# Two transformer layers on one core: pace of the row maxima, order of some loads, last block's rows kept on chip, banks of the first scores

## Chip, cores and metric

The kernel runs on one core of a Trainium2 chip. The metric is the device time of one execution in microseconds. Times are medians of several runs; one further execution is profiled, and all traces below are of such executions.

## What is computed

Two pairs of layers on an input of 2048 rows and 640 columns, in float32. Each pair is an attention layer and an MLP, both added to their input, with the same weights in both pairs:

```python
x = x + A(layernorm(x))     # D = 640, 32 heads of 20, softmax over 2048 keys
x = x + B(layernorm(x))     # F = 1536, squared relu, two biases
...                         # once more

def A(x):
    qkv = (x @ wqkv).reshape(1, 2048, 3, 32, 20)
    p = softmax(einsum("bhqd,bhkd->bhqk", q, k) * 20 ** -0.5)
    return einsum("bhqk,bhkd->bhqd", p, v) @ wo

def B(x):
    h = x @ w1 + b1
    return where(h > 0, h, 0) ** 2 @ w2 + b2
```

## The kernel before

**Stages.** `layer` is called twice. Each call runs three stages one behind the other: `qkv` (the projections, by blocks of 512 rows), `attention`, and the output projection with the MLP (`add_heads` for four row blocks, then `mlp` for four). Most products are made of three products of float32r pieces ("high" and "low"). Between stages the pieces of q, k, v and of the weights lie in DRAM and come by DMAs issued on the SP queue, in the order of the program.

**Order.** All instructions are issued by a schedule written out in Python. Each engine works through its own instructions in that order, and waits where another engine or a DMA isn't done. PSUM has eight banks. Rings hand them out in turn: `ps_st` (banks 0 to 3) for scores, `ps_q` (0 to 3) for maxima and transposes in `qkv`, `ps_pj` (4 to 7) for projections, `sm_ring` (4, 5, 6) for maxima in the attention, `ps_all` (all eight) in the rest.

**Projections.** `qkv` goes through 72 chains, 40 for queries and keys (`UNITS`, by row block `tb` and position) and 32 for values, each of 15 products on both halves of the rows of the array. Between their matmuls it inserts other work, chosen by a model of the engines' time (`now`, with `READY` and 0.235 us for a step): transposes of the next row block (`turns`), and maxima of the first attention blocks. `step_rest` advances a generator that loads and normalises the next rows; when it hands over a `turns` generator, that is queued with the model time from which it may run. In layer two the rows of blocks 0 to 2 come turned through DRAM already; block 3 is loaded again (`second`, with `rows_of_block` and `prepare`: statistics of four rows, then normalising of four) and turned by TensorE. At the end of a value chain `end_v` copies the bank to `v` (line 377). When the last chain is two thirds through, the first four scores are issued (`for o in "abab"`).

**Attention.** 32 blocks `t` of four heads by 512 queries, each with 16 key tiles. The scores are made a second time by queries, ahead of use, to find each row's maximum: a matmul in `smax` (line 481) and a reduction on VectorE (line 493); the negated maxima go through DRAM into two rows of `q` (`mrows`, `mrows_load`; names `nm`, `mr`, `d_m`), where line 563 adds them into the score. Some maxima are taken in pairs during `qkv` ("double", line 510). The others are spread over the attention. It works in groups of eight key tiles; a group's order is a string of `ORDERS`, chosen by how many pairs of maxima it has to hold (12 to 16):

```python
12: "naambbmVanmbambVbmannabVnabnmabVabnmbanVbbmnanaVbmmbaanVbmbmnaaV",
```

`a` and `b` are scores of the two heads in the two halves of the array, with the exponential on ScalarE behind each (line 570); `m` and `n` are maxima in the two halves; `V` is the product with the values for one key tile (line 575). `pairs` chooses the number: it takes the pace at which the maxima of each block would be done in time, adds it to a debt, and takes whole pairs from the debt. The last block is done with scores two banks wide (`both_heads`, lines 1089 and 1096).

**Behind the attention.** `add_heads` has four row blocks of eight chains (line 293, 15 matmuls each); VectorE adds each to a row tile `x` (line 1164), which was loaded one block ahead. After each chain `side` runs one of the queued `steps`; they normalise and turn block 0 for the MLP: `turn_out` writes turned rows to `d_t`, `turn_in` loads them (`xnT<-d_t`) and splits them on ScalarE (line 1212) and VectorE or Pool (line 1213). The weights of the MLP are loaded there too: `loads` gives each block its own (w_1 has 15 slots of 512 KB at most, w_2 16). `mlp` adds the second product to its rows on VectorE (line 1260) and stores them; the last tile in two halves.

Of the kernel before, what the change touches and what calls it, by code (L numbers as in the profile page):

```python
# [11 lines left out]
ALU = mybir.AluOpType  # L12
# [13 lines left out]
NQB = S // QB  # L26
NG = H // 4
NKT = S // P
# [11 lines left out]
def tile_layers(  # L40
# [11 lines left out]
    nc = tc.nc  # L52
# [17 lines left out]
    def dma(eng, dst, src):  # L70

        if dst.dtype == F32R:
            dst = dst.bitcast(F32)
        if src.dtype == F32R:
            src = src.bitcast(F32)
        eng.dma_start(dst, src)  # L76

    def xtile(label):
        return xpool.tile([P, D], F32, tag="x", name=name(label))

    banks = psum.tile([P, 8, 512], F32, tag="banks", name="banks")
# [14 lines left out]
    ps_st = Ring(0, 1, 2, 3)  # L96
    ps_pj = Ring(4, 5, 6, 7)
    ps_q = Ring(0, 1, 2, 3)
# [102 lines left out]
    w_1 = Split("w1", P, NF * 2 * KD)  # L201
# [170 lines left out]
    def end_v(tt, hf, dst):  # L372
        whole = tt in vs
        if not whole:
            vs[tt] = slot([P, H, 32], F32, "v")
            nc.gpsimd.memset(vs[tt][:, :, DH:], 1.0)
        nc.scalar.copy(
            vs[tt][:, hf * 16 : hf * 16 + 16, :DH],
            dst[:, :HALF].rearrange("p (h d) -> p h d", d=DH),
        )  # L380
        if whole:
            v = vs.pop(tt)
            return lambda: dma(nc.sync, d_v[tt * P : (tt + 1) * P], v)

    def rows_of_block(tb, x_src):
        return [row_tile(x_src, tb * 4 + i) for i in range(4)]
# [156 lines left out]
    def mrows_load(t):  # L543
# [7 lines left out]
            )  # L551
        done.add(t)

    def score(t, kt, h, es):

        p, par = divmod(h, 2)
        if p not in es:
            es[p] = weights[len(e_n) % len(weights)]
            e_n.append(t)
        dst = ps_st("st")  # L560
        b = 64 * par
        assert t in done
        nc.tensor.matmul(  # L563
            dst,
            k_t[t // NQB, kt // 4][b : b + 62, p, (kt % 4) * P : (kt % 4 + 1) * P],
            q_t[t][b : b + 62, p, :],
            start=True,
            stop=True,
        )
        nc.scalar.activation(es[p][:, par, :], dst, AF.Exp, scale=SCALE)  # L570
# [111 lines left out]
    def qkv(first, x_src, rest, scores):  # L682
# [157 lines left out]
        def step_rest():  # L840
            cost, turn = next(rest, None) or (0, None)
            if cost:
                now["dve"] = max(now["dve"], now["pe"]) + cost
            if turn:
                turning.append((now["dve"] + READY, turn))

        def step_turn():
            if next(turning[0][1], None) is None:
# [115 lines left out]
    def attention(first, x_src, first_rows):  # L964
# [135 lines left out]
        def pairs():  # L1100

            n, i = min(sm_n), state["begun"] + 1
            most = max(
                [8 * (e + 1 - n) / max(t * NKT - 5 - i, 1) for t, e in ends.items() if e >= n],
                default=0,
            )
            state["debt"] += most
            n = min(max(round(state["debt"]), 12), 16)
            state["debt"] -= n
            return n  # L1110

        for o in "abab":
            op(o)
        yield
# [101 lines left out]
    def new_rows():  # L1216
        return [slot([P, 2, QB], F32R, "xnT") for _ in range(KD)]

    def mlp(qb, xnt, x_mid, x_dst, side):

        xs = []
        for fh in range(2):
            hs = []
            for f in range(fh * 6, fh * 6 + 6):
                dst = ps_all("pu")
                chain(dst, [
                    (w_1.piece(f * 10 + hw * KD + k), xnt[k][:, hx, :])
                    for k in range(KD)
                    for hw, hx in THREE
                ])  # L1230
                if qb == NQB - 1:
                    w_1.past(f * 10 + 9)
                r = xtile("r")[:, :QB]
                nc.scalar.activation(r, dst, AF.Relu, bias=b1_t[:, f : f + 1])  # L1234
                nc.vector.tensor_mul(r, r, r)  # L1235
                h = slot([P, 2, QB], F32R, "h")
                split_to(h[:, 0, :], h[:, 1, :], r)
                hs.append(h)
                if fh == 0 and f in (1, 2, 3, 4):
                    x = row_tile(x_mid, qb * 4 + f - 1)  # L1240
                    nc.gpsimd.tensor_add(x, x, b2_t)
                    xs.append(x)
                side()
            f0 = fh * 6

            def part(dst, hf, i, fs):
                for f in fs:
                    for hx, hw in THREE:
                        nc.tensor.matmul(  # L1249
                            dst[:, :HALF],  # L1250
                            hs[f][:, hx, i * P : (i + 1) * P],
                            w_2.piece(at_2(f0 + f, hw, hf)),
                            start=(f == 0 and (hx, hw) == THREE[0]),
                            stop=(f == 5 and (hx, hw) == THREE[-1]),
                        )

            def add(dst, hf, i):
                c = slice(hf * HALF, (hf + 1) * HALF)
                x = xs[i]
                nc.vector.tensor_add(x[:, c], dst[:, :HALF], x[:, c])  # L1260
                r0 = (qb * 4 + i) * P
                if fh == 1 and qb * 4 + i == NKT - 1:
                    dma(nc.sync, x_dst[r0 : r0 + P, c], x[:, c])
                elif fh == 1 and hf == 1:
                    dma(nc.sync, x_dst[r0 : r0 + P, :], x)
                side()

            first_two = [ps_all("y") for _ in range(2)]
            for fs in (range(5), (5,)):
                for i in range(2):  # L1270
                    part(first_two[i], 0, i, fs)
            for i in range(2):
                add(first_two[i], 0, i)
            for hf in range(2):
                for i in range(0 if hf else 2, 4):
                    dst = ps_all("y")
                    part(dst, hf, i, range(6))
                    add(dst, hf, i)
            if fh == 0 and qb == NQB - 1:
                w_2.past(at_2(5, 1, 1))  # L1280

    def layer(first, x_a, x_m, x_e, front_0, ahead):
# [15 lines left out]
        def all_steps():  # L1298
# [3 lines left out]
        xnt, rows = [], []  # L1302
        loads = [
            [(w_1, s) for s in range(8)],
            [(w_1, s) for s in range(8, w_1.n)],
            [(w_2, s) for s in range(5)],
            [(w_2, s) for s in range(5, 10)],
        ]
        for qb in range(NQB):
            if qb + 2 == NQB:  # L1310
                xnt.extend(new_rows())
            add_heads(qb, x_a, x_m, xs, side, rows)
            if qb == 0:
                out_0 = turn_out(d_t[0], rows)
                steps.extend([lambda: next(out_0)] * 10)
                in_0 = turn_in(d_t[0], lambda: xnt)
                steps.extend([lambda: next(in_0)] + [None] * 2 + [lambda: next(in_0)] * 5)
            for sp, s in loads[qb]:
                sp.load(s)
            if qb + 1 == NQB:  # L1320
                all_steps()
# [3 lines left out]
        for qb in range(NQB):  # L1325
            new = []
            plan = [[] for _ in range(28)]

            def put(gen, *sides):
                for i in sides:  # L1330
                    plan[i].append(lambda: next(gen))

            def rows_of(src, tb):
                return lambda i: row_tile(src, tb * 4 + i)

            def to(where):

                def get():
                    where.extend(new_rows())
                    return where  # L1340

                return get

            d = d_t[(qb + 1) % 2]
            if qb + 1 < NQB:
                put(turn_out(d, rows_of(x_m, qb + 1)), *range(4, 14))
                put(turn_in(d, to(new)), 19, *range(22, 27))
            if ahead and qb:
                out_at = range(14, 24) if qb + 1 < NQB else range(2, 12)
                put(turn_out(d_t[1 + qb], rows_of(x_e, qb - 1)), *out_at)  # L1350
            if ahead and qb + 1 == NQB:
                for tb, at in enumerate((4, 14, 19)):
                    xt_[tb] = []
                    sub = nc.gpsimd.tensor_sub if tb == 2 else nc.vector.tensor_sub
                    put(turn_in(d_t[2 + tb], to(xt_[tb]), sub), at, *range(at + 3, at + 8))
                for n in range(5):
                    plan[20 + n].append(lambda n=n: w_qk.load(n))
            steps.extend((lambda p=p: [f() for f in p]) for p in plan)
            mlp(qb, xnt, x_m, x_e, side)
            xnt = new  # L1360
            if qb + 1 < NQB:
                all_steps()
# [4 lines left out]
    def second():  # L1367


        x = rows_of_block(3, d_x[1])  # L1370
        yield 0, None
        yield from prepare(x, turns(3, x, ps_q, (1, 3)))

    def constants():

# [102 lines left out]
```

## Time and profile before

| what | us |
|---|---|
| median of 3 runs | 3593.64 |
| lowest and highest | 3592.02, 3597.27 |
| profiled execution | 3596.07 |
| span of that execution, first to last instruction | 3594.3 |
| busy: TensorE / VectorE / ScalarE / Pool | 3576.5 / 2755.3 / 2649.0 / 805.5 |

Layer one: projections to about 313 us, attention to about 1400, the rest to about 1809; layer two then the same. In the lines of the profile PE is TensorE, PEld its weight load, DVE VectorE, ACT ScalarE, POOL GpSimd, SPq the DMA queue of SyncE. A line of the timeline has its start, its length, the engine, the line of the kernel, the operation, what is written and read, and the count; in square brackets stands how long the engine was idle before it, and what ended that. A line of the busy times by stretch has the ends of the stretch, its length, the busy time of each engine with its instructions, the granted clock of TensorE, the busy share of the DMA engines and GB/s.

### The profile page before, as it was taken

Reading aid. Unit: us, or ns where it says so; the run is one execution under the profiler, and the core shown is the slowest. Engines: PE = TensorE matmul, PEld = TensorE weight load, DVE = VectorE, ACT = ScalarE, POOL = GpSimd, SP = SyncE. Lnnn points to the kernel's source line nnn. Section 1 sums busy time; section 2 is a strip of 40 time slices with the busy share of each in tenths; the row PEclk is TensorE's granted clock in tenths of the full one; section 3 lists DMA queues with packets and bytes.
Section 4 is the critical chain, followed back from the end, with each engine's and each line's share of the span. In section 5 each row is a group of like instructions: output and inputs, shape, how many; then the busy total and the mean of one; then the engine's idle time right before and its main releaser. Section 6 shows DMA issues by size and latency. Waiting matters only on the chain.

```text
span 3594.3 us, 67684 instructions
## 1 busy us (share of the span) xinstructions
PE 3576.5 (100%) x25560; PEld 2127.4 (59%) x25560; DVE 2755.3 (77%) x5081; ACT 2649.0 (74%) x5150; POOL 805.5 (22%) x880
## 2 busy tenths in 40 slices
PE   9999999999999999999999999999999999999999
PEld 7896343443434335999988964334343343369998
DVE  8878999999999993445567789999999999924443
ACT  3778999999999995122227789999999999942221
POOL 6531434211211211111243201211211211211110
PEclk9999999999999999999999999999999999999999
DMA  9765555323211126834477652232222211367221
GB/s 305 273 228 166 168 153 158 104 69 77 60 44 51 50 89 204 262 86 121 134 265 253 204 150 69 67 78 55 73 72 62 49 40 51 105 214 250 74 79 39
DMA packets 378118, 453.89 MB, mean 126 GB/s; under 512 B 176723, under 2 KB 224083, under 8 KB 377791
## 3 DMA queue, kind: packets, MB, share of 16 engines
q1 hardware_dynamic: 376974, 447.21, 41.6%
q8 instruction: 201, 3.29, 0.4%
q10 hardware_dynamic: 816, 2.36, 0.2%
q14 instruction: 127, 1.03, 0.1%
HBM read 275.14 MB, written 174.30 MB: 125 GB/s over the span
## 4 chain that ended last, share of the span: by engine, by line
PE 95%; DVE 1%; DMA 1%; ACT 1%; issue 1%; POOL 1%; SPq 0%; ACTq 0%; DVEq 0%; POOLq 0%
PE banks L575 28%; PE banks L563 19%; PE banks L481 16%; PE banks L293 13%; PE banks L1249 9%; PE banks L331 9%; DMA q<-d_qk 1%; PE banks L1089 1%; ACT e L570 0%; DVE bst L244 0%; SPq L76 0%; DVE x L252 0%; ACT e L1096 0%; DVE xnT L257 0%; DMA d_qk<-ev 0%
## 5 line engine op out<-in xcount | busy, mean ns | idle before, releaser
L570 ACT ACTIVATE e<-banks 128x512 f32<-128x512 f32 x3968 | 2049.2, 603 | 66.7 <-PE banks L563 6.9
L493 DVE TENSOR_REDUCE mx<-banks 128x1 f32<-128x512 f32 x3076 | 1931.0, 685 | 206.9 <-PE banks L481 132.0
L481 PE MATMUL banks<-k,q 60*128 60x512 f32 x3586 | 1243.0, 428 | 2.7 <-DVE mx L493 1.4
L563 PE MATMUL banks<-q,k 62*128 62x512 f32 x3968 | 1116.1, 433 | 0.9 <-DVE mx L510 0.9
L575 PE MATMUL banks<-e,vg 128*32 128x512 f32 x8192 | 1091.0, 605 | 1.5 <-ACT e L1096 1.5
L563 PEld LDWEIGHTS banks<-q,k 62*128 62x128 f32 x3968 | 583.7, 185 | 654.6 <-ACT e L570 622.5
L481 PEld LDWEIGHTS banks<-k,q 60*128 60x128 f32 x3586 | 581.5, 184 | 292.6 <-DVE mx L493 219.4
L510 DVE CUSTOM_DVE_ANT_0 rl<-banks,rl 128x512 f32<-128x512 f32 x510 | 332.8, 689 | 101.1 <-PE banks L481 91.6
L331 PE MATMUL banks<-xnT,wqk 64*128 64x512 f32 x2400 | 379.9, 394 | 0.6 <-ACT mark_t L333 0.6
L575 PEld LDWEIGHTS banks<-e,vg 128*32 128x32 f32 x8192 | 161.1, 108 | 357.2 <-issue 331.2
L1234 ACT ACTIVATE r<-banks,b_t 128x512 f32<-128x512 f32 x96 | 66.2, 690 | 400.6 <-PE banks L293 400.6
L502 ACT ACTIVATE rl<-banks 128x512 f32<-128x512 f32 x510 | 270.9, 597 | 98.8 <-PE banks L481 94.6
L1249 PE MATMUL banks<-w,h 128*128 128x320 f32 x2304 | 340.4, 309 | 0.0
L1249 PEld LDWEIGHTS banks<-w,h 128*128 128x128 f32 x2304 | 339.1, 188 | 1.3
L293 PE MATMUL banks<-xnT,w 128*128 128x512 f32 x1440 | 329.4, 389 | 0.0
L331 PEld LDWEIGHTS banks<-xnT,wqk 64*128 64x128 f32 x2400 | 285.6, 185 | 35.6 <-issue 2.4
L293 PEld LDWEIGHTS banks<-xnT,w 128*128 128x128 f32 x1440 | 269.6, 188 | 55.3
L271 POOL CAST mr<-nt 128x32 fp32r<-128x32 f32 x64 | 13.5, 211 | 1117.7 <-DVE nt L536 1117.6
L619 POOL TENSOR_TENSOR few<-few,minus_t 128x16 f32<-128x16 f32 x62 | 179.9, 2901 | 231.2 <-DMA few<-d_s 231.2
L331 PE MATMUL banks<-wv,xnT 64*128 64x320 f32 x1920 | 199.1, 307 | 0.9 <-ACT mark_t L333 0.9
L331 PEld LDWEIGHTS banks<-wv,xnT 64*128 64x128 f32 x1920 | 186.7, 185 | 2.5 <-ACT mark_t L333 1.4
L1235 DVE TENSOR_TENSOR r<-r 128x512 f32<-128x512 f32 x96 | 75.6, 787 | 125.4 <-ACT r L1234 124.0
(82 smaller groups left out, 2019.4 us busy)
## 6 DMA issues: line engine op xcount, KB each, us to landing
q<-d_qk SPq DMA_DIRECT2D x242, 240.0 KB
d_qk<-ev SPq DMA_DIRECT2D x80, 512.0 KB
k<-d_qk SPq DMA_DIRECT2D x152, 240.0 KB
x<-d_x SPq DMA_DIRECT2D x88, 320.0 KB
d_qk<-ev SPq DMA_DIRECT2D x80, 256.0 KB
d_o<-ot SPq DMA_DIRECT2D x248, 80.0 KB
ot<-d_o SPq DMA_DIRECT2D x38, 512.0 KB
d_v<-v SPq DMA_DIRECT2D x32, 512.0 KB
```

The lines of the kernel that those rows point to most:

```text
L293: nc.tensor.matmul(dst, a, b, start=(n == 0), stop=(n == last))
L331: m = nc.tensor.matmul(ch["dst"][:, :width], *pair, start=first, stop=last)
L481: nc.tensor.matmul(dst, q_t[t][b : b + 60, p, sub * P : (sub + 1) * P], k_t[t // NQB, c][b : b + 60, p, :], start=True, stop=True,)
L493: nc.vector.tensor_reduce(maxima(t)[:, 2 * par + p, sub, c : c + 1], dst, axis=AX.X, op=ALU.max)
L502: nc.scalar.activation(res, dst, AF.Relu)
L510: nc.vector.tensor_tensor_reduce(out=r, in0=dst, in1=r, scale=1.0, scalar=LEAST, op0=ALU.add, op1=ALU.max, accum_out=maxima(t)[:, 2 * par ...
L563: nc.tensor.matmul(dst, k_t[t // NQB, kt // 4][b : b + 62, p, (kt % 4) * P : (kt % 4 + 1) * P], q_t[t][b : b + 62, p, :], start=True, stop ...
L570: nc.scalar.activation(es[p][:, par, :], dst, AF.Exp, scale=SCALE)
L575: nc.tensor.matmul(acc[32 * h : 32 * h + 32, :], v_t[t // NQB, kt // 8][:, kt % 8, 32 * h : 32 * h + 32], es[p][:, par, :], start=(kt == 0 ...
L619: nc.gpsimd.tensor_tensor(few, few, minus_t, op=ALU.pow)
L1235: nc.vector.tensor_mul(r, r, r)
L1249: nc.tensor.matmul(dst[:, :HALF], hs[f][:, hx, i * P : (i + 1) * P], w_2.piece(at_2(f0 + f, hw, hf)), start=(f == 0 and (hx, hw) == THREE[0]),
```

## The change

Six edits. (1) `pairs` reckons the end of a block's maxima two key tiles later (3 for 5) and rounds the debt down. (2) The first two scores of an attention take banks 5 and 6; the ring `ps_st` begins with the third. (3) The last value tile is copied by VectorE, not ScalarE. (4) The second part of w_1 (slots 8 to 14) is loaded from a step behind the loads of the turned rows, not at the end of block 1. (5) In layer one the MLP's last row block stays on chip: after each of its last additions it takes the statistics of that row and normalises the one before into a new tile `y`; `second` normalises the last and hands over the transposes with its first step, and loads nothing. The halved store of the last tile stays in layer two alone. (6) Turning may not begin before the model time of about one chain.

```diff
-        nc.scalar.copy(
+        (nc.vector.tensor_copy if tt == NKT - 1 else nc.scalar.copy)(
             vs[tt][:, hf * 16 : hf * 16 + 16, :DH],
...
+    free = []
+
     def score(t, kt, h, es):
...
-        dst = ps_st("st")
+        dst = banks[:, free.pop(0), :] if free else ps_st("st")
...
             if turn:
-                turning.append((now["dve"] + READY, turn))
+                turning.append((max(now["dve"] + READY, N * 0.235 - 0.1), turn))
...
             most = max(
-                [8 * (e + 1 - n) / max(t * NKT - 5 - i, 1) for t, e in ends.items() if e >= n],
+                [8 * (e + 1 - n) / max(t * NKT - 3 - i, 1) for t, e in ends.items() if e >= n],
                 default=0,
             )
             state["debt"] += most
-            n = min(max(round(state["debt"]), 12), 16)
+            n = min(max(int(state["debt"]), 12), 16)
...
+        free.extend((5, 6))
         for o in "abab":
             op(o)
...
+    rows_3 = []
+
+    def to_normal(x, mv):
+        y = xtile("y")
+        nc.vector.tensor_scalar(y, x, mv[:, 0:1], mv[:, 1:2], op0=ALU.subtract, op1=ALU.mult)
+        return y
+
-    def mlp(qb, xnt, x_mid, x_dst, side):
+    def mlp(qb, xnt, x_mid, x_dst, side, last):
...
-                if fh == 1 and qb * 4 + i == NKT - 1:
+                if fh == 1 and last and qb * 4 + i == NKT - 1:
                     dma(nc.sync, x_dst[r0 : r0 + P, c], x[:, c])
                 elif fh == 1 and hf == 1:
                     dma(nc.sync, x_dst[r0 : r0 + P, :], x)
+                    if not last and qb + 1 == NQB:
+                        rows_3.append((x, stats(x)))
+                        if i:
+                            rows_3[i - 1] = to_normal(*rows_3[i - 1])
...
         loads = [
             [(w_1, s) for s in range(8)],
-            [(w_1, s) for s in range(8, w_1.n)],
+            [],
...
-                steps.extend([lambda: next(in_0)] + [None] * 2 + [lambda: next(in_0)] * 5)
+                steps.append(lambda: next(in_0))
+                steps.append(lambda: [w_1.load(s) for s in range(8, w_1.n)])
+                steps.extend([None] + [lambda: next(in_0)] * 5)
...
-            mlp(qb, xnt, x_m, x_e, side)
+            mlp(qb, xnt, x_m, x_e, side, not ahead)
...
     def second():
-        x = rows_of_block(3, d_x[1])
-        yield 0, None
-        yield from prepare(x, turns(3, x, ps_q, (1, 3)))
+        rows_3[3] = to_normal(*rows_3[3])
+        yield 0.65, turns(3, rows_3, ps_q, (1, 3))
```

## The prediction

> **What bounds the kernel now.** I read the busy times of the page first, then the list of waits for TensorE alone, and last the timeline and the busy times by stretch at the places that the diff touches.
>
> ```profile
> PE 3576.5 (100%) x25560; PEld 2127.4 (59%) x25560; DVE 2755.3 (77%) x5081; ACT 2649.0 (74%) x5150; POOL 805.5 (22%) x880
> PE banks L293 <- DVE x L1164: 2.6, 1, 2.6
> ```
>
> The first row is of the page, the second of the list of waits (us in total, times, longest). TensorE is busy 3576.5 of 3594.3 us, so only 17.8 us of its idle time can be won. What can be won beside it is time in which PE counts as busy but goes slowly: matmuls spread out by waits of a few tenths, or a halved clock. A saving on another engine counts only where it reaches PE.
>
> **Maxima per group.** The attention works in groups of eight key tiles, each with a fixed order of scores (a, b), maxima (m, n) and value products (V). The view of busy time by stretch, cut to the matmuls of the maxima (line 481), shows the groups; the ends of a stretch are starts of value products.
>
> ```profile
> core 0: us, PE busy (x) PEld busy (x), PEclk, DMA share, GB/s
> 312.00:1372.00 1060.00, 500.76 (x1476) 233.24 (x1476) 1.00 0.34 95
> 2102.00:3158.00 1056.00, 500.68 (x1472) 233.18 (x1472) 1.00 0.26 68
> 450.19:485.98 35.79, 16.41 (x51) 7.77 (x50) 1.00 0.64 174
> 502.96:536.94 33.98, 16.31 (x49) 7.57 (x48) 1.00 0.49 158
> 791.74:827.54 35.80, 16.42 (x51) 7.78 (x50) 1.00 0.18 47
> 1133.40:1169.16 35.76, 16.42 (x51) 7.77 (x50) 1.00 0.13 34
> 2495.11:2530.37 35.26, 16.56 (x51) 7.77 (x50) 1.00 0.35 86
> ```
>
> Layer one has 1476 maxima here, or 738 pairs, layer two 736. Two groups with 24 pairs take 33.98 us; the two that hold 25 take 35.79, 35.80 and 35.76 in layer one and 35.26 in layer two. One thirteenth pair thus costs 1.81, 1.82, 1.78 and 1.28 us.
>
> By the old formula, layer one begins with 8 x 738 / (496 - 5 - 1) = 12.049 pairs a group. The debt grows by about 0.05 a group and round() lifts a group to 13 when it passes 0.5: the tenth, thirtieth and fiftieth, as the trace shows; in layer two (8 x 736 / 490 = 12.016) one. With 3 for 5 it is 8 x 738 / 492 = 12.000 in layer one, and stays 12.000 as both terms shrink; int() needs a whole pair of debt, and none gathers. Layer two has 11.967. Of all blocks the last one (31) always gives the largest quotient. So all four groups of 13 go: 5.41 + 1.28 = 6.7 us.
>
> The pairs aren't gone. Of 738, 61 groups take 732, and the 62nd takes 6 instead of 3; in layer two 4 instead of 3.
>
> ```profile
> 344.13:361.10 16.97, 16.97 (x124) 6.78 (x120) 15.87 (x28) 16.46 (x33) 4.30 (x5) 1.00 0.43 108
> 1356.42:1372.70 16.28, 16.21 (x104) 5.33 (x104) 4.39 (x9) 16.09 (x31) 0.50 (x3) 1.00 0.21 56
> 1360.90 0.22 DVE L525 TENSOR_REDUCE nm<-mx 128x16 f32<-128x64 f32 x1
> 1361.74 1.16 SPq L76 DMA_DIRECT2D d_m<-mr  x2
> 1364.36 0.53 SPq L76 DMA_DIRECT2D q<-d_m  x2
> 1369.63 1.07 PE L1089 MATMUL banks<-q,k 62*128 62x512 f32 x4
> ```
>
> A full group takes 16.97 us, the 62nd 16.28 (all engines: PE, PEld, DVE, ACT, POOL). Its three more pairs put three of eight tiles from the lower to the higher pace: 0.69 x 3/8 = 0.3 us, and 0.1 for one pair in layer two. Net: **-6.3 us**, between -4.5 (each pair given back at the full 1.3 to 1.8 us for one group) and -6.9.
>
> The same shift makes the negated maxima of the last block late. In the order for 12 the third pair ends ahead of the third V, the sixth ahead of the fourth, one tile or 16.97 / 8 = 2.1 us later. From nm at 1360.90 to the read q<-d_m at 1364.36 is 3.5 us; the write before it took 2.6 us from its issue to the read's release, which I take for the read too, so it lands at 1367.0, and 2.1 us to 2.7 (with one reduce more in front) later at 1369.1 to 1369.7. The first wide scores (1369.63) move to about 1369.9. It just fits: 0 to 1 us, taken as +0.2.
>
> **Weights behind the turned rows.** The timeline of layer one, with a row of the DMA issues ahead and two of the chain of waits (those with x420 and x90):
>
> ```profile
> w<-d_w SPq DMA_DIRECT2D x30, 512.0 KB
> 1404.21 61.61 PE banks L293 x420
> 1444.89 3.08 SPq L76 DMA_DIRECT2D d_t<-y  x4
> 1448.63 4.34 SPq L76 DMA_DIRECT2D w<-d_w  x7
> 1454.56 8.38 SPq L76 DMA_DIRECT2D d_t<-y  x4
> 1465.21 2.22 SPq L76 DMA_DIRECT2D xnT<-d_t  x5
> 1468.76 0.62 ACT L1212 CAST xnT<-xnT 128x512 fp32r<-128x512 f32 x1 [58.37 <-DMA xnT<-d_t]
> 1469.41 0.69 DVE L1213 TENSOR_TENSOR xnT<-xnT 128x512 fp32r<-128x512 f32 x1 [18.48 <-ACT xnT L1212]
> 1470.56 6.20 PE L293 MATMUL banks<-wo,ot 128*128 128x320 f32 x30 [2.55 <-DVE x L1164]
> 1470.56:1474.05 3.49, 3.49 (x13) 3.49 (x14) 2.58 (x5) 2.41 (x4) 0.00 (x0) 0.51 0.96 369
> 1518.31 20.43 PE banks L293 x90
> ```
>
> SP issues seven loads of 512 KB, then the last four stores of turned rows, which take 8.38 us behind the weights (3.08 for the four ahead of them), then the loads of xnT. VectorE is in order and stands 18.48 us at the first subtraction of xnT; the additions behind it hold eight banks, and TensorE runs dry for 2.55 us. The clock granted in the 3.49 us behind that is 0.51. The stall costs 2.55 + 0.49 x 3.49 = 4.26 us. It happens once: the wait of line 293 above counts one, so layer two has none.
>
> After the change the seven loads (4.34 us on SP alone, and 7 x 0.524 MB at 369 GB/s = 9.9 us of transfer) follow xnT. So xnT comes at least 4.3 us earlier, more than the gap, and the gap goes. What is late next: the residual rows of the last block, two of which now stand behind the weights on SP's queue and land up to 9.9 us later. VectorE waits for them, and TensorE goes on for eight banks, eight chains of 15 matmuls at 61.61 / 420 = 0.147 us, 17.6 us; that covers it. Slots 8 and up of these weights are wanted from the second half of the first MLP block on, at 1518. **-4.3 us** in layer one, 0 in layer two; between 0 (other executions may not have the gap, or it moves) and -4.3.
>
> The page "TensorE: Matmul & The Clock Gate" of the Trainium skill (Part 1) says that the clock halves after an idle window of about 3.4 us. Here a pause of 2.55 us sufficed; by the page's length the 1.7 us of slow clock would not be sure in each execution, and the total would be 1.7 us higher.
>
> **Last block's rows kept on chip.** The timeline at the border of the layers:
>
> ```profile
> 1793.56 5.98 POOL L1213 TENSOR_TENSOR xnT<-xnT 128x512 fp32r<-128x512 f32 x4
> 1794.48 1.39 DVE L1213 TENSOR_TENSOR xnT<-xnT 128x512 fp32r<-128x512 f32 x1
> 1809.12 0.49 DVE L1260 TENSOR_TENSOR x<-banks,x 128x320 f32<-128x320 f32 x1 [2.15 <-PE banks L1249]
> 1813.65 0.89 DVE L244 BATCH_NORM_STATS2 bst<-x 128x6 f32<-128x320 f32 x2 [4.03 <-DMA x<-d_x]
> 1817.68 3.09 DVE L252 TENSOR_SCALAR x<-x,mv 128x640 f32<-128x640 f32 x4
> 1818.36 0.96 POOL L248 TENSOR_TENSOR mv<-mv,half_t 128x1 f32<-128x1 f32 x1
> 1812.98 6.65 PE L331 MATMUL banks<-xnT,wqk 64*128 64x512 f32 x56 [0.28 <-ACT mark_t L333]
> 1820.82 0.77 PE L408 MATMUL banks<-ident,x 128*128 128x128 f32 x5 [0.71 <-DVE x L252]
> ```
>
> Gone: four loads, with 4.03 us of VectorE's waiting. Moved into the last four additions of the MLP: statistics (1813.65 to 1817.68 for four rows, 1.0 each) and normalising (3.09 / 4 = 0.8), 1.8 us beside 0.49 of addition, under the 2.64 us that lie between additions (0.49 + 2.15). The last row is added by 1809.6 and has its statistics by 1810.6. Its two Pool steps took until 1819.32, 1.6 us behind the statistics, so 1812.2 here, and it is normalised by 1813.0. The transposes now follow the first chain's 15 steps, which end at 1812.7 (1812.98 - 0.28), and reach the last row just then. Of the pauses (0.28 + 0.71) some 0.2 stays: **-0.8 us**, between -1.4 and +3 (rival 2).
>
> **First scores and value copies.** Timeline, layer one and then two:
>
> ```profile
> 310.21 0.69 DVE L510 CUSTOM_DVE_ANT_0 rl<-banks,rl 128x512 f32<-128x512 f32 x1 [0.24 <-PE banks L481]
> 310.96 0.50 PE L563 MATMUL banks<-q,k 62*128 62x512 f32 x2 [0.45 <-DVE mx L510]
> 312.51 0.76 ACT L377 COPY v<-banks 128x320 f32<-128x320 f32 x2
> 2101.60 0.50 PE L563 MATMUL banks<-q,k 62*128 62x512 f32 x1 [0.45 <-DVE mx L510]
> ```
>
> By the draws from the ring of four (587 in layer one, 1168 in layer two) the last double maximum lies in bank 3 and in bank 0, the one before it in 2 and 3. The four scores took 1, 2, 3, 0. In layer one the third waited for bank 3. With 5, 6, 1, 2 only bank 2 is in question, free at 309.97 (310.21 - 0.24), so the last two scores start near 310.2, not 310.96: -0.8 us. In layer two the ring, two draws behind, gives 5, 6, 3, 0: the fourth score waits as before, 0. The two value copies cost VectorE about 2 x 0.49 us (as its addition of 128x320) and ScalarE 0.76 less; VectorE sat idle there, and the maximum that follows needs the copied bank on either engine. **-0.8 us**, between 0 and -1.5. The turning's new lower bound changes nothing in layer one, whose rows are later by the planner's own clock.
>
> **Sum.** -6.3 + 0.2 - 4.3 - 0.8 - 0.8 = -12.0 us. The profiled execution took 3596.07 us (1.8 around its span) and would take 3584.1; the median of the runs before, 3593.64, is 2.4 lower, so 3581.6.
>
> **Rivals.**
> 1. The weights are late for something else. If TensorE had to wait out all seven loads in both layers, 2 x 9.9 = 19.8 us come and the 4.3 stay lost: 3593.6 - 7.7 + 19.8 = 3605.7, slower. It decides once residual rows land more than 17.6 us behind their chain. The cover of eight banks speaks against it; that the DMA engines are full there (share 0.96) speaks for it. 0.06.
> 2. The rows' work collides with Pool. The VectorE subtraction beside Pool's four took 1.39 us, elsewhere 0.69. The last Pool subtractions (5.98 / 4 = 1.5 us each) now stand between the statistics' Pool steps; if two of them delay the last row, it is 3 us late and the transposes wait: +3 in place of -0.8, 3585.4. 0.15. The page "SBUF — State Buffer" of the Trainium skill (Who interferes with whom) says that of two such operations of VectorE and GpSimd the later one blocks for the whole of the earlier. The 1.39 us agrees.
> 3. The stall of 2.55 us is of this one execution, or comes back elsewhere: 3593.6 - 7.7 = 3585.9. 0.15.
> 4. The planner does not do what it says: groups of 13 stay, or the last block's rows come so late that the wide scores wait a tile and a half (3 us) in both layers. Either eats the groups' 6.1 us: 3587.7. 0.06.
>
> **How the numbers follow.** The forecast has 0.58. A measurement of this kernel can tell about 0.2%, 7.2 us, from no change. The forecast and rivals 2 and 3 lie beyond that (12.0, 8.2 and 7.7 us), 0.88 together, but with a second term short they don't, for which I take off 0.08: faster 0.80. Same: those 0.07 and rival 4, 0.13; slower: rival 1 and the last 0.01, 0.07. Range: all terms at their better ends give -6.9 - 4.3 - 1.4 - 1.5 = -14.1, and with 1.6 for the spread of the runs (the lowest before is 3592.02) 3578.0; on the other side rivals 2 and 3 both in full give 3589.7, so 3590.0, which holds rival 4 too.
>
> **What would show it.** Right: 24 pairs (x48) in each two groups, at 33.98 us; xnT's loads issued more than 4 us earlier behind the attention, no wait at line 293, a granted clock of 1.00 there; no x<-d_x at the border and transposes right behind the first 30 matmuls; the wait for L510 gone in layer one, still there in layer two. Wrong: x50 in any two groups; a wait of L1089 for q<-d_m; a wait at L408 over 1 us; a new gap at L293 or L1249.

## Result: 12 us less, and the profile after

| | before | after |
|---|---|---|
| median, beside each other (6 runs each) | 3595.16 | 3582.98 |
| lowest to highest | 3592.02 to 3597.27 | 3582.15 to 3583.51 |
| profiled execution | 3596.07 | 3583.33 |
| its span | 3594.3 | 3581.5 |

The ratio is 0.9968, with an interval of 0.9958 to 0.9978: 12.2 us less (7.9 to 15.1 by the interval). Against the first median of before (3593.64) it is 10.7 us. These six runs of before spread over some 5 us, those of after over 1.4; in the 25 runs of before that stand beside experiments 1, 3, 4 and 8 it is 10 (3591.45 to 3601.80).

The page of the kernel after begins with the span and the busy times:

```profile
span 3581.5 us, 67667 instructions
...
PE 3569.0 (100%) x25560; PEld 2121.6 (59%) x25560; DVE 2753.5 (77%) x5085; ACT 2647.3 (74%) x5146; POOL 805.2 (22%) x880
```

Of the list of waits for TensorE (us in total, times, longest) three rows bear on the change:

```profile
PE banks L481 <- DVE mx L493: 0.6, 1, 0.6
PE banks L565 <- DVE mx L510: 0.4, 1, 0.4
...
PE banks L408 <- DVE x L252: 0.3, 1, 0.3
```

TensorE's idle time fell from 17.8 to 12.5 us, and its busy time by 7.5 us with the same number of matmuls: the larger part was time in which PE counted as busy and went slowly. The row of line 293 is gone from the waits; that of the maxima's banks (L481 behind L493) went from 2.2 us to 0.6, that of the first scores (now L565) from two waits to one.

The table shows where the time went, from the two profiled executions (us; a negative difference is time saved). A stage reaches from the first matmul of its kind to the first of the next; the attention from its first value product to the end of its last.

| stage | before | after | difference | forecast |
|---|---|---|---|---|
| projections of q and k, layer one | 195.00 | 194.59 | -0.41 | |
| first value chain to first value product, layer one | 106.59 | 105.63 | -0.96 | -0.8 |
| attention, layer one | 1087.20 | 1081.78 | -5.42 | -4.9 |
| output projection, layer one | 72.96 | 68.60 | -4.36 | -4.3 |
| MLP of layer one | 332.41 | 332.42 | 0 | |
| projections of q and k, layer two | 188.23 | 187.17 | -1.06 | -0.8 |
| first value chain to first value product, layer two | 106.77 | 106.87 | +0.10 | 0 |
| attention, layer two | 1083.10 | 1082.56 | -0.54 | -1.2 |
| output projection, layer two | 68.64 | 68.60 | -0.04 | |

Four views of after answer to those of before. First the busy time by stretch of the maxima's matmuls, over both attentions, and over two groups each in layer one and in layer two, at the places where 25 pairs stood before:

```profile
310.80:1370.40 1059.60, 501.27 (x1476) 233.62 (x1476) 1.00 0.34 96
2090.10:3146.10 1056.00, 501.10 (x1472) 233.19 (x1472) 1.00 0.26 68
448.91:482.90 33.99, 16.27 (x49) 7.60 (x48) 1.00 0.68 183
2483.23:2517.20 33.97, 16.28 (x49) 7.59 (x48) 1.00 0.34 83
```

The counts of both attentions are what they were, so no pair is gone; two groups hold 24 pairs (48 weight loads) and take 33.99 and 33.97 us, where they held 25 and took 35.79 and 35.26. Then the timeline behind the attention of layer one: SP's issues, VectorE's, and TensorE's first chains of the MLP.

```profile
1441.81 3.32 SPq L76 DMA_DIRECT2D d_t<-y  x4
1447.37 2.22 SPq L76 DMA_DIRECT2D xnT<-d_t  x5
1449.63 4.88 SPq L76 DMA_DIRECT2D w<-d_w  x7
1451.67 0.69 DVE L1216 TENSOR_TENSOR xnT<-xnT 128x512 fp32r<-128x512 f32 x1 [7.39 <-ACT xnT L1215]
1466.55 0.89 DVE L1167 TENSOR_TENSOR x<-banks,x 128x320 f32<-128x320 f32 x2 [8.88 <-DMA x<-in_A_x_dram]
1465.60 9.71 PE L293 MATMUL banks<-xnT,w 128*128 128x512 f32 x42
```

And the busy time by stretch of the whole output projection there (all engines):

```profile
1396.99:1465.60 68.61, 68.61 (x468) 68.37 (x467) 29.54 (x56) 3.63 (x6) 2.97 (x8) 1.00 0.89 285
```

The four stores take 3.32 us instead of 8.38, xnT's loads are issued at 1447.37 instead of 1465.21 (11.2 us earlier, counted from the start of the stage, which itself begins 6.65 us earlier), VectorE stands 7.39 us at them instead of 18.48, and the stretch has TensorE busy from end to end at a clock of 1.00. What was named as late next is there too: VectorE waits 8.88 us for a residual row, and TensorE, with eight banks ahead, shows no pause.

The border of the layers:

```profile
1798.12 0.49 DVE L1270 TENSOR_TENSOR x<-banks,x 128x320 f32<-128x320 f32 x1 [0.53 <-PE banks L1259]
1800.83 0.61 DVE L1226 TENSOR_SCALAR y<-x,mv 128x640 f32<-128x640 f32 x1 [0.71 <-POOL mv L248]
1798.01 3.71 PE L331 MATMUL banks<-xnT,wqk 64*128 64x512 f32 x30
1801.65 1.09 PE L408 MATMUL banks<-ident,y 128*128 128x128 f32 x8
```

The normalising of the last row begins 2.7 us after its addition did; the transposes follow the first 30 matmuls with no wait, and the loads are gone. Last, the start of the attention in layer one and in layer two:

```profile
309.94 0.69 DVE L510 CUSTOM_DVE_ANT_0 rl<-banks,rl 128x512 f32<-128x512 f32 x1 [0.24 <-PE banks L481]
310.93 0.89 DVE L377 COPY v<-banks 128x320 f32<-128x320 f32 x2 [0.28 <-PE banks L331]
312.53 1.07 PE L577 MATMUL banks<-e,vg 128*32 128x512 f32 x8
2089.53 0.50 PE L565 MATMUL banks<-q,k 62*128 62x512 f32 x1 [0.44 <-DVE mx L510]
2092.05 1.06 PE L577 MATMUL banks<-e,vg 128*32 128x512 f32 x8
```

In layer one no score waits for a double maximum any more; in layer two the fourth still waits 0.44 us.

### The profile page after: what moved, and what is told of

Read it like the earlier page. It is cut to its first block, busy times and chain, and to the rows that moved or that the text cites. A ratio compares the mean times of both kernels' runs of the same rounds, so it can differ in the third digit from the quotient of the medians.

```text
span 3581.5 us, 67667 instructions
## 1 busy us (share of the span) xinstructions
PE 3569.0 (100%) x25560; PEld 2121.6 (59%) x25560; DVE 2753.5 (77%) x5085; ACT 2647.3 (74%) x5146; POOL 805.2 (22%) x880
## 3 DMA queue, kind: packets, MB, share of 16 engines
q10 hardware_dynamic: 816, 2.36, 0.2%
## 4 chain that ended last, share of the span: by engine, by line
PE 96%; DVE 2%; DMA 1%; issue 0%; ACT 0%; POOL 0%; SPq 0%; ACTq 0%; DVEq 0%
PE banks L577 28%; PE banks L565 20%; PE banks L481 16%; PE banks L293 13%; PE banks L331 10%; PE banks L1259 9%; DVE mx L493 1%; PE banks L1091 1%; DMA q<-d_qk 0%; ACT e L1098 0%; DVE bst L244 0%; DVE xnT L257 0%; DVE x L252 0%; DMA d_qk<-ev 0%; PE banks L408 0%
## 5 line engine op out<-in xcount | busy, mean ns | idle before, releaser
L493 DVE TENSOR_REDUCE mx<-banks 128x1 f32<-128x512 f32 x3076 | 1929.6, 683 | 208.4 <-PE banks L481 137.2
L481 PE MATMUL banks<-k,q 60*128 60x512 f32 x3586 | 1244.3, 427 | 1.0 <-DMA q<-d_qk 0.5
L565 PE MATMUL banks<-q,k 62*128 62x512 f32 x3968 | 1118.7, 434 | 0.4 <-DVE mx L510 0.4
L565 PEld LDWEIGHTS banks<-q,k 62*128 62x128 f32 x3968 | 584.4, 185 | 657.8 <-ACT e L572 625.6
L481 PEld LDWEIGHTS banks<-k,q 60*128 60x128 f32 x3586 | 582.0, 184 | 283.1 <-DVE mx L493 210.8
```

The source lines that it names most:

```text
L481: nc.tensor.matmul(dst, q_t[t][b : b + 60, p, sub * P : (sub + 1) * P], k_t[t // NQB, c][b : b + 60, p, :], start=True, stop=True,)
L493: nc.vector.tensor_reduce(maxima(t)[:, 2 * par + p, sub, c : c + 1], dst, axis=AX.X, op=ALU.max)
L565: nc.tensor.matmul(dst, k_t[t // NQB, kt // 4][b : b + 62, p, (kt % 4) * P : (kt % 4 + 1) * P], q_t[t][b : b + 62, p, :], start=True, stop ...
```

## Experiments

The kernels of experiments 1, 3, 4 and 8 ran beside before at a median of 3594.65 us (25 runs), those of 2, 5, 6 and 7 beside 3594.69 (22 runs). After itself ran beside a median of before of 3595.16, so a difference to after that is given below compares batches whose medians of before lie up to 0.5 us apart. "After less" means that one edit of the change is undone; "before plus" that one is made alone.

### 1. After, less the new pace

```diff
-                [8 * (e + 1 - n) / max(t * NKT - 3 - i, 1) for t, e in ends.items() if e >= n],
+                [8 * (e + 1 - n) / max(t * NKT - 5 - i, 1) for t, e in ends.items() if e >= n],
-            n = min(max(int(state["debt"]), 12), 16)
+            n = min(max(round(state["debt"]), 12), 16)
```

> The changed kernel with the old pace of the maxima (5 for 3, round() for int()). If the groups of 25 maxima in 35.3 to 35.8 us are what the change took away (theory of the prediction), three of them come back in layer one and one in layer two: the first attention is 5.4 us longer, the second 0.5 to 1.3, together 3583.0 + 6 to 6.7 = 3589 to 3589.7 us. Rival: the pairs cost the same wherever they are done, and the first attention became shorter by its better start: less than 1.5 us comes back.

Measured: 3589.91 us (3589.17 to 3590.83 but for one stray execution of 4558; 11 runs), 0.9983 of before (0.9974 to 0.9993), so 6.9 us above after. Layer one's attention takes 1087.61 us, as before the change, and layer two's 1083.25. The busy time by stretch of the maxima, over the same groups as above:

```profile
448.85:484.63 35.78, 16.43 (x51) 7.78 (x50) 1.00 0.64 174
2489.04:2524.27 35.23, 16.53 (x51) 7.78 (x50) 1.00 0.33 85
```

From its list of waits for TensorE:

```profile
PE banks L481 <- DVE mx L493: 2.5, 5, 0.6
```

The groups of 13 are back at their old price, and with them the waits for the maxima's banks. The pace is the largest part of the gain, as said. The two halves of this edit (3 for 5, and int() for round()) were not tried apart; by the prediction's own quotient of 12.000 the first alone would leave no group of 13 in layer one.

### 2. Before, with another order for 13 pairs

Why does one pair more cost 1.8 us, when its two matmuls keep TensorE busy for some 0.34 us each (501.27 / 1476)? Either the order written out for 13 is a bad one, or a group can't bear 25 or 26 maxima.

```diff
-        13: "baanmbVmbanambbnbmVanbmnaVnaabnmbVanbmaanVnmbbanaVmnbmabVabbmmnaVm",
+        13: "naambbmVanmbambVbmannabVnmabnmabVabnmbanVbbmnanaVbmmbaanVbmbmnaanV",
```

> The kernel before, with another order for groups of 13: the order for 12 with one m and one n put in. The groups of 13 stay where they were. Theory S: most of the 1.3 to 1.8 us that a group of 13 took is the old order's (one tile of 3.3 us), and with this order such a group costs 0.3 to 0.6 us more than one of 12; the attentions are 3.6 to 4.4 us and 0.7 to 1 us shorter than before, total about 5 us less. Theory P: a thirteenth pair overloads VectorE, whose reductions fill 91% already, and costs the same in any order: no change from the kernel before.

Measured: 3594.39 us (3591.13 to 3597.95; 11 runs), a ratio of 1.0 (0.9991 to 1.001). In the trace a group of 13 costs 1.4 us instead of 1.8 in layer one, and layer one's attention falls from 1087.20 to 1086.30. In layer two it costs 1.4 as well, a little more than the 1.3 of the old order there. Two tiles now hold four maxima; they take 2.94 and 2.73 us instead of 2.12. The timeline around the first of them:

```profile
471.21 1.07 PE L575 MATMUL banks<-e,vg 128*32 128x512 f32 x8
472.74 2.48 DVE L493 TENSOR_REDUCE mx<-banks 128x1 f32<-128x512 f32 x4 [0.21 <-PE banks L481]
473.49 0.50 PE L481 MATMUL banks<-k,q 60*128 60x512 f32 x1 [0.32 <-DVE mx L493]
474.15 1.06 PE L575 MATMUL banks<-e,vg 128*32 128x512 f32 x8
```

And the busy time by stretch of the maxima over the two groups, in layer one and in layer two:

```profile
449.96:485.36 35.40, 17.20 (x51) 7.93 (x50) 1.00 0.66 176
2490.73:2526.13 35.40, 17.22 (x51) 7.92 (x50) 1.00 0.35 84
```

The two groups take 35.40 us instead of 35.79 in layer one, and instead of 35.26 in layer two. The tile with four maxima reaches from the value product at 471.21 to the next at 474.15. Four reductions take VectorE 2.48 us, more than a tile of 2.12; the fourth maximum has to wait for the reduction of the bank that it takes, three back in the ring of three (started at 472.74, over at 473.43), and the scores behind it wait in TensorE's queue. So neither theory holds as it was put: the order has a share in layer one (0.4 of 1.8) and none in layer two, but the larger part stays with an order built like that for 12, in which a tile that holds four maxima is longer. Whether a still better order exists is open. Dropping the pair from the group, as the change does, saves what no order tried here does.

### 3. After, with the weights in their old place

```diff
-                steps.append(lambda: [w_1.load(s) for s in range(8, w_1.n)])
+                steps.append(None)
...
-            [],
+            [(w_1, s) for s in range(8, w_1.n)],
```

> The changed kernel with the second part of w_1 loaded where it was, ahead of the last turned rows. Theory: the wait of the output projection for the turned rows comes back in layer one, 2.5 us and some 1.7 us of halved clock, so 4.3 us in an execution that has it. The six runs of the kernel before lie in two clusters, 3592.0 to 3593.6 and 3596.7 to 3597.3, which is about this amount apart; so I expect two clusters here too, at 3583.0 to 3584 and at 3587 to 3587.5. Rival: the wait had another cause that the other edits took away: one cluster at 3583.

Measured: 3586.76 us (3584.98 to 3588.12; 9 runs), 0.9977 of before (0.9967 to 0.9986), 3.8 us above after. The expected two clusters did not come: the runs lie all over 3 us, and the 25 runs of before beside them show no two clusters either. Its profile shows the stall, smaller than before's. From the timeline, a row of SP and one of TensorE:

```profile
1446.33 8.28 SPq L76 DMA_DIRECT2D d_t<-y  x4
1463.18 3.04 PE L293 MATMUL banks<-wo,ot 128*128 128x320 f32 x19 [1.69 <-DVE x L1167]
```

The busy time by stretch in the 4 us behind it (all engines, then the granted clock):

```profile
1463.18:1467.18 4.00, 4.00 (x27) 4.00 (x28) 4.00 (x9) 1.24 (x2) 0.00 (x0) 1.00 1.04 399
```

The same view of before, behind its pause:

```profile
1470.64:1474.05 3.41, 3.41 (x13) 3.41 (x14) 2.58 (x5) 2.41 (x4) 0.00 (x0) 0.50 0.97 373
```

The four stores behind the weights take 8.28 us again. The pause is 1.69 us and the clock behind it stays at 1.00; before, the pause was 2.55 us and the clock 0.50 for 3.41 us. The output projection takes 70.55 us here, 68.60 after, 72.96 before. In the kernel of experiment 2, which loads in the old order too, the pause is 1.08 us and the stage takes 69.96. None of the seven profiles with the new order has the pause. So the order of the queue makes the stall, but its size is a matter of the execution: 1.4 to 4.4 us in the three profiles. In layer two the same stage takes 68.64 us in before, 69.01 here and 69.10 in experiment 2, and 68.60 in all seven with the new order: there too the old order can cost a few tenths.

### 4. Before, with the weights moved alone

> The kernel before with the move of the second part of w_1 alone. Theory: no wait of line 293 in either layer, and all runs in one cluster at the lower end of the kernel before, 3591.5 to 3593; the profile's stretch from the first projection chain to the MLP is 68.6 us in layer one too, not 73. Rival: the transfer is as late for the residual rows, the stretch stays over 70 us, and the runs stay spread to 3597.

The diff is the fourth edit of the change and nothing else. Measured: 3592.21 us (3590.19 to 3593.95; 11 runs), 0.9992 of before (0.9983 to 1.0001): 2.4 us less, but the interval just includes no change. In its profile the wait of line 293 is gone and the output projection takes 68.60 us, as expected. The runs spread over 3.8 us, more than expected, so the stall is not the only thing that varies. With experiment 3 the estimate for the move is 2.4 to 3.8 us in the median; the 4.36 of the table is that of one execution with a large stall.

### 5. After, with the last block's rows loaded again

```diff
-            mlp(qb, xnt, x_m, x_e, side, not ahead)
+            mlp(qb, xnt, x_m, x_e, side, True)
...
-        rows_3[3] = to_normal(*rows_3[3])
-        yield 0.65, turns(3, rows_3, ps_q, (1, 3))
+        x = rows_of_block(3, d_x[1])
+        yield 0, None
+        yield from prepare(x, turns(3, x, ps_q, (1, 3)))
```

> The changed kernel, but the last block's rows of layer two are loaded again and normalised there, as before. Theory: the two pauses of TensorE at the border (0.28 and 0.71 us) come back: first query-key chain to first value chain of layer two 188.2 us in place of 187.2, total 3584.0. Rival: that stretch is bound by the stores and loads of q and k behind it, and nothing comes back: 3583.0.

Measured: 3584.86 us (3583.53 to 3586.28; 9 runs), 0.9973 of before (0.9963 to 0.9983), 1.9 us above after in the median. The wait for the rows is back in its timeline, and the first transposes with their waits:

```profile
1801.34 0.89 DVE L244 BATCH_NORM_STATS2 bst<-x 128x6 f32<-128x320 f32 x2 [3.45 <-DMA x<-d_x]
1801.28 6.65 PE L331 MATMUL banks<-xnT,wqk 64*128 64x512 f32 x56 [0.28 <-ACT mark_t L333]
1808.69 0.77 PE L408 MATMUL banks<-ident,x 128*128 128x128 f32 x5 [0.29 <-DVE x L252]
```

The stage takes 187.72 us against 187.17 after. Over all ten profiles it is 187.80 on the mean of the four kernels that load the rows (188.23, 187.72, 187.32, 187.92) and 186.93 on that of the six that keep them (187.17, 186.81, 186.54, 187.03, 187.31, 186.69): -0.9 us. The rest of the 1.9 has no place in the stages, and lies within the spread of these runs.

### 6 and 7. After, less one of the two edits at the start

Experiment 6 leaves out the free banks, experiment 7 the copies on VectorE:

```diff
-        free.extend((5, 6))
```

```diff
-        (nc.vector.tensor_copy if tt == NKT - 1 else nc.scalar.copy)(
+        nc.scalar.copy(
```

> The changed kernel with the first two scores on the ring again. Theory: layer one's third score waits for the last double maximum once more, and its start is 0.8 to 1.0 us later; layer two is unchanged: 3583.8 to 3584.0. Rival: the start moved because ScalarE was rid of the value copies, and nothing changes: 3583.0.

> The changed kernel with the last value tile's copies on ScalarE again. Theory: they are neither here nor there: VectorE has 0.9 us less, ScalarE 0.8 us more, and the third maximum waits for the copied bank in both; within 0.3 us of 3583.0. Rival: ScalarE was the limit of the start, and each layer's first value product is 0.5 us later: 3584.0.

Measured: 3584.33 us without the banks (3583.9 to 3586.03; 7 runs; 0.9971 of before, 0.996 to 0.9982) and 3584.18 without the copies (3583.49 to 3585.08; 7 runs; 0.997, 0.9959 to 0.9981). Both are about 1.3 us above after, at the edge of what can be told; the stages say more. In experiment 7 it was the rival that came in layer one, whose first value product is 0.55 us later; in layer two the stage grew by 0.13 only. From the first value chain to the first value product, layer one takes:

| | copies on ScalarE | copies on VectorE |
|---|---|---|
| scores from bank 1 on | 106.59 (before) | 106.42 (experiment 6) |
| scores from 5, 6 | 106.18 (experiment 7) | 105.63 (after) |

The banks alone give -0.41, the copies alone -0.17, both -0.96. The stage repeats well: it takes 106.59 to 106.64 us in the three kernels that have neither edit (before, experiments 2 and 4) and 105.60 to 105.65 in the five that have both (after, experiments 1, 3, 5 and 8). The timelines of layer one show why. Experiment 6:

```profile
310.64 0.51 PE L565 MATMUL banks<-q,k 62*128 62x512 f32 x2 [0.45 <-DVE mx L510]
313.28 1.07 PE L577 MATMUL banks<-e,vg 128*32 128x512 f32 x8
```

Experiment 7:

```profile
310.32 2.07 ACT L572 ACTIVATE e<-banks 128x512 f32<-128x512 f32 x4 [0.77 <-issue]
312.24 0.79 ACT L377 COPY v<-banks 128x320 f32<-128x320 f32 x2
313.08 0.50 PE L481 MATMUL banks<-k,q 60*128 60x512 f32 x1
313.51 1.07 PE L577 MATMUL banks<-e,vg 128*32 128x512 f32 x8
```

In 6 the third score waits for bank 3. In 7 the scores are early, but ScalarE makes the copies only behind the four exponentials, and the maximum that takes the copied bank starts at 313.08, when they are done. Each wait hides part of the other, so taking one away alone gives less than half of both.

### 8. After, with the ring of the first scores two draws on in layer two

```diff
         free.extend((5, 6))
+        if not first:
+            ps_st.n += 2
```

> The changed kernel, and in layer two the ring of the score banks is moved on by two, so that the four scores take banks 5, 6, 1, 2 as in layer one, not 5, 6, 3, 0. Theory: the fourth score's wait for the last double maximum (0.44 us) goes and the rest of the chain starts 0.8 us earlier: values to first value product in layer two 106.0 us in place of 106.9, total 3582.2. Rival: the start isn't set by TensorE but by the exponentials or by VectorE's backlog, and the 0.8 us is lost within the first tiles: total 3583.0.

Measured: 3583.56 us (3581.37 to 3583.76; 5 runs), 0.9966 of before (0.9953 to 0.9978), not told apart from after. The start of layer two takes 106.12 us against 106.87, near the 106.0 expected, and the wait of L565 for the double maximum is gone from the list. But the attention of layer two takes 1083.00 us against 1082.56. In the five other kernels with the new pace it takes 1082.25 to 1082.91, so most of that may be spread; whether some of the 0.75 was given back there, and by what, was not followed up. No kernel here had a lower median than the one after.

## Why the prediction held, and where it did not

The forecast was 3581.6 us with a range of 3578 to 3590; 3582.98 lies in it. The sum of -12.0 us for the profiled execution compares with -12.7.

**Groups, layer one: right.** -5.42 us in the stage for a net of -4.9; the price by two groups, the number of groups and the cause (a debt that no longer gathers a pair) were as read. The 62nd group went from 16.28 to 16.48 us, +0.2 where 0.3 was reckoned. The 0.2 for late scores of the last block was not needed: the read of the rows was issued at 1360.87 and the first wide scores came at 1363.14, with no wait. That the stage comes so near the forecast is partly luck: the first tile of block 28 takes 2.13 us where it took 2.51, a saving of 0.38 that the prediction doesn't name. It takes 2.49 to 2.51 in all four profiles with the old pace and 2.12 to 2.14 in all six with the new one. In before, at 1270.8, two small operations of VectorE (lines 525 and 536, 0.21 us each) stand there right behind a copy of 0.68 us and ahead of six reductions; with the new pace they are elsewhere. After's busy time in the 62nd group, and its timeline there:

```profile
1349.70:1366.18 16.48, 16.27 (x108) 5.66 (x107) 8.08 (x15) 16.26 (x31) 0.81 (x3) 1.00 0.21 56
```

```profile
1360.87 0.53 SPq L76 DMA_DIRECT2D q<-d_m  x2
1363.14 0.73 PE L1091 MATMUL banks<-q,k 62*128 62x512 f32 x4
```

**Groups, layer two: mis-sized.** The term was -1.28 + 0.1 = -1.2; the stage gave -0.54. The group of 13 did go, for 1.29 us. The step that failed is that of the pairs "given back": it counted them only at the end of the attention (44.53 us became 44.69, as reckoned), and left out that the new pace also moves the point where a block's maxima are complete. There VectorE has two small operations more, between the maxima, in after at 2954.2:

```profile
2954.21 0.21 DVE L525 TENSOR_REDUCE nm<-mx 128x16 f32<-128x64 f32 x1
2954.52 0.21 DVE L536 STREAM_TRANSPOSE nt<-nm 128x32 f32<-128x32 f32 x1
2954.66 3.66 DVE L493 TENSOR_REDUCE mx<-banks 128x1 f32<-128x512 f32 x6
2956.55 0.18 PEld L481 LDWEIGHTS banks<-k,q 60*128 60x128 f32 x1 [0.40 <-DVE mx L493]
2957.22 1.07 PE L577 MATMUL banks<-e,vg 128*32 128x512 f32 x8
```

They push six reductions into one run, a weight load waits 0.40 us for a bank, and this tile takes 2.36 us instead of 2.12. The same tile takes 2.36 to 2.38 in all six profiles with the new pace (after, experiments 3, 5, 6, 7 and 8) and is not long in the four without it, so it belongs to the pace. Another 0.19 lies in the second tile of the layer (2.31 instead of 2.12), where VectorE comes from the value copies behind a late fourth score; experiment 7, with the copies on ScalarE, and experiment 8, with no late score, don't show it, while experiment 1, with the old pace, does (2.33), so this part belongs to the copies. So -1.29 + 0.16 + 0.24 + 0.19 = -0.70. The mean of the six profiles with the new pace is 0.75 below that of before and experiments 1 and 4 (1082.61 against 1083.36), so what is left beside the -0.54 is within the spread of executions.

**Weights: the mechanism right, the size that of one execution.** Table and forecast agree to 0.1 us, because both were made on the same execution of before, with its pause of 2.55 us. In the medians the move is worth 2.4 to 3.8, by experiments 4 and 3. So rival 3 was right in part: the stall comes in every profile with the old order, but mostly smaller. The forecast's median has the same fault in it: it took a fixed 2.4 us from profile to median, where after's profiled run lies 0.35 above its own. A smaller stall explains only part of this: the kernel of experiment 4 has no stall in its profile, and its runs still spread over 3.8 us.

The row of the clock was read rightly against the page "TensorE: Matmul & The Clock Gate" of the Trainium skill (Part 1), which has the clock halve after an idle window of about 3.4 us: a pause of 2.55 us did it here, and the measurement decides. That the clock then stays low for 3.41 us agrees with the length that the page gives for the window. The pauses of 1.69 and 1.08 us left the clock at 1.00; nothing here shows where between 1.69 and 2.55 the point lies, or whether it is fixed. One thing the clock records of the ten traces do show: the stretches at full clock last whole multiples of 3.413 us (in before 1464.32 and 2119.68, 429 and 621 times that; in after 3577.17, 1048 times). Counted on in such steps from the first rise of the clock, each of the three pauses lies within a single step, so how long a pause must be when it falls across two steps is open too.

**Rows kept on chip: right.** -0.9 us by the ten profiles, for -0.8. Rival 2 did not come: Pool's subtractions were over in time, and VectorE waited 0.71 us for Pool's step of the last row, within the 3.7 us of the first chain.

**First scores and copies: right sum, wrong account.** The -0.8 was put to the banks alone, and the copies were costed at nothing. The copies on ScalarE were a wait of their own behind that of the banks. What failed is the sentence that the maximum needs the copied bank on either engine: it does, but on ScalarE the copies stand behind four exponentials, and end at 313.03 in experiment 7, where VectorE's end at 311.82 in after. Layer two was right: the fourth score waits as before, and experiment 8 shows that the ring's position is why.

**Rivals 1 and 4** are refuted by the rows above: no wait for the weights or residual rows on TensorE in either layer, no group of 13, and no late scores.

The opening and the projections of layer one gave some 0.3 us that no step of the prediction names. The projections of layer one take 194.65 to 195.08 us in the three profiles without the sixth edit and 194.01 to 195.04 in the seven with it, so this can't be told from the spread; the sixth edit was not tried alone, and its effect is open.

## What to carry to other kernels

Filler work that is spread over groups should be levelled so that no group holds more than its banks and its slowest engine bear; one pair over cost 1.3 to 1.8 us here, about two to nearly three times what its two matmuls keep TensorE busy, and most of that counted as busy time, not as a wait. On a queue that issues in order, put bulk loads behind the small transfers that somebody waits for, and check how many banks cover what becomes late in turn. When two waits end at nearly the same point, try them together as well as one by one: here each alone gave less than half.

## Not expected

- A stall whose cause lies fixed in the queue's order had pauses of 2.55, 1.69 and 1.08 us in three executions, and only the longest also halved the clock. One profile sizes such a term badly.
- Four maxima in a tile of 2.12 us lengthen it by 0.6 to 0.8 us, though VectorE's four reductions (2.48 us) exceed it by 0.36 only. That three banks are too few to carry the rest into the next tile is the likely reason; no run had more banks in the ring.
- Two operations of 0.21 us on VectorE, at the wrong place between reductions, lengthened a tile of TensorE's by 0.24 us in layer two of after, and, as the timeline reads, by 0.38 in layer one of before.
